# The layer norm at the start of a decode step's backward kernel moved to ScalarE, and its large clears divided between two engines

## The chip, the cores and the metric

The kernel runs on one core of one Trainium2 chip. The metric is the device time of one execution in microseconds (us), here the median of several runs. A profile records one further execution, in which every engine's instructions and every transfer have a start and a duration. TensorE is called PE, its weight load PEld, VectorE DVE, ScalarE ACT, GpSimd POOL and SyncE SP, as in the profile.

## The reference

The computation is one decode step of a transformer block, forward and backward together. Batch is 2, sequence 1, width D = 576; there are 32 query heads and 16 key/value heads of 128, a cache of 4096 positions, and a bilinear MLP of width F = 4608.

```python
def _layernorm(x, axis=-1, eps=1e-5):
    m = jnp.mean(x, axis=axis, keepdims=True)
    v = jnp.var(x, axis=axis, keepdims=True)
    return (x - m) / jnp.sqrt(v + eps)

def _A_ref(x, k_cache, v_cache, wq, wo):        # 2 query heads for each key/value head
    q = (x @ wq) as [B, Hq, 1, Dh]
    scores = einsum("bhqd,bhkd->bhqk", q, k) * (Dh ** -0.5)
    o = einsum("bhqk,bhkd->bhqd", softmax(scores), v)
    return o as [B, 1, Hq * Dh] @ wo

def _B_ref(x, w_gate, w_up, w_down):
    return ((x @ w_gate) * (x @ w_up)) @ w_down

xn = _layernorm(x)
out = x + _A_ref(xn, ...) + _B_ref(xn, ...)
```

The kernel returns `out` and its gradients, for the given `grad_out`, with respect to x, both caches, and the five weight matrices. The two cache gradients alone are 67 MB, as large as the caches that are read. All told 92.5 MB are read and 92.5 MB written.

## The kernel before

**Constants and the front.** A front of small work comes first. POOL clears `ident`, `xs`, `Wdy`, `W` (two of them), `dM`, `Wm`, `Wt`, `oT` and `rowT`, that is, stationary operands of which later steps overwrite only a part. DVE derives a dozen selection matrices from the identity (`identf`, `sel`, `selA`, `R4`, `G4`, `RV`, `F8`, `Q4`, `C32`, `mask8`, `maskc`; lines 130 to 159). The layer norm of the two rows of x then works on [2, 576] tiles: a cast to `x_f` (line 168), the row sum `mu` (171), the mean (172), the centred `xn_f` (174), its mean square `var` (177), `rstd` by ACT's square root (184) and DVE's reciprocal (185), the scaling (186), and the cast to `xn_bf` (188). PE spreads `dy_bf` and `xn_bf` over all partitions (`dyr`, `xnr`, lines 198 to 200) and transposes `xn_bf` into `xs` (207 to 212). `Wdy` is filled from the transposed `dyr` (220).

**Groups.** Four groups of four key/value heads follow. `group_loads` loads a slice of the query weights `wq` and of the output weights `wo`; `group_front` makes from them the query rows and the rows of the output's gradient (`qd`, lines 458 to 476, with `Wdy` as weights of the `wo` matmuls) and spreads them (`rep`, 485). `build_W` (496, POOL) puts them into the cleared `W`.

**Steps.** Each of the 16 steps handles two heads of one batch: it loads K (1 MB a head, line 520), transposes it on DVE (`X`, helper line 121), computes scores on PE (`ps_sc`), the softmax, then loads V and does the same for the probabilities' gradient. At the end of a step `contract` multiplies the probabilities with V (and their gradient with K one step later). The cache gradients are outer products that PE forms in `ps_o`; ACT or DVE evicts them (`so`, helper lines 112 and 109), and POOL issues their stores (585). Nine slices of the MLP are interleaved as units between them (`mlp_units`: `wgu` and `wd` are loaded at 316 to 319).

**What sets the order.** A tile framework schedules the instructions from the program's order and priorities; on each engine they run strictly in the order that it wrote out. All loads go through SP's queue in one order. The loaded tiles (`wq`, `wo`, `wgu`, `wd`, `kv`, and in the front `xn_f`) share 12 buffers of the tag `nat`, so that a load is issued only when the last reader of the tile that held its buffer is done; SP then stands at that load, and all later loads stand behind it:

```python
    def nat(shape, name):
        return sb.tile(list(shape), BF16, tag="nat", bufs=12, name=name)
```

Of the kernel before, what the change touches and what calls it, by code (L numbers as in the profile page):

```python
# [8 lines left out]
AF = mybir.ActivationFunctionType  # L9
ALU = mybir.AluOpType  # L10
AX = mybir.AxisListType
FP32 = mybir.dt.float32
# [11 lines left out]
def kernel(  # L24
# [22 lines left out]
    nc = tc.nc  # L47

    Bq, Sq, D = A_x.shape
# [20 lines left out]
    const = ctx.enter_context(tc.tile_pool(name="const", bufs=1))  # L70
# [86 lines left out]
    for be in range(4):  # L157
# [5 lines left out]
    x_bf = sb.tile([2, D], BF16, tag="st", bufs=5, name="x_bf")  # L163
# [1 line left out]
    dy_bf = sb.tile([2, D], BF16, tag="st", bufs=5, name="dy_bf")  # L165
    nc.sync.dma_start(dy_bf[:], grad_out.rearrange("b s d -> (b s) d"))
    x_f = sb.tile([2, D], FP32, tag="X", bufs=3, name="x_f")
    nc.vector.tensor_copy(x_f[:], x_bf[:])

    mu = const.tile([2, 1], FP32, name="mu")  # L170
    nc.vector.reduce_sum(mu[:], x_f[:], axis=AX.X)
    nc.vector.tensor_scalar(mu[:], mu[:], 1.0 / D, None, op0=ALU.mult)
    xn_f = sb.tile([2, D], FP32, tag="nat", bufs=12, name="xn_f")
    nc.vector.tensor_scalar(xn_f[:], x_f[:], mu[:], None, op0=ALU.subtract)
    xsq = sb.tile([2, D], FP32, tag="X", bufs=3, name="xsq")
    var = const.tile([2, 1], FP32, name="var")
    nc.vector.tensor_tensor_reduce(
        out=xsq[:], in0=xn_f[:], in1=xn_f[:], scale=1.0 / D, scalar=0.0,
        op0=ALU.mult, op1=ALU.add, accum_out=var[:],
    )  # L180
    eps_t = const.tile([2, 1], FP32, name="eps_t")
    nc.vector.memset(eps_t[:], EPS)
    rstd = const.tile([2, 1], FP32, name="rstd")
    nc.scalar.activation(rstd[:], var[:], AF.Sqrt, bias=eps_t[:], scale=1.0)
    nc.vector.reciprocal(rstd[:], rstd[:])
    nc.vector.tensor_scalar(xn_f[:], xn_f[:], rstd[:], None, op0=ALU.mult)
    xn_bf = sb.tile([2, D], BF16, tag="st", bufs=5, name="xn_bf")
    nc.vector.tensor_copy(xn_bf[:], xn_f[:])


    sel2 = const.tile([2, 4, 32], BF16, name="sel2")
# [21 lines left out]


    Wdy = const.tile([P, NB, 2, P], BF16, name="Wdy")
    nc.gpsimd.memset(Wdy[:], 0.0)
    dyT = sb.tile([P, 2 * NB, 32], BF16, tag="X", bufs=3, name="dyT")
    t32(dyT[:].rearrange("p k m -> p (k m)"), view(dyr[:], 0, P, 0, [[64, NB], [1, 2], [2, 32]]))
    for a in range(4):
# [2 lines left out]

    W = [const.tile([P, 4, 2, WW], BF16, name=f"W{t}") for t in range(2)]
    dM = const.tile([P, 2, 2, P], BF16, name="dM")
    for t in range(2):
        nc.gpsimd.memset(W[t][:], 0.0)
    nc.gpsimd.memset(dM[:], 0.0)
    Wms = [const.tile([P, 35, 8], BF16, name=f"Wm{i}") for i in range(2)]
    Wts = [const.tile([P, 19, 8], BF16, name=f"Wt{i}") for i in range(2)]
    oTs = [const.tile([P, 2, GH, 32], BF16, name=f"oT{i}") for i in range(2)]  # L230
# [693 lines left out]
```

## Time and profile before

| quantity | before |
|---|---|
| median of 5 runs | 520.44 us (518.93 to 536.76) |
| the 5 runs | 536.76, 520.44, 519.57, 531.47, 518.93 us |
| profiled execution: time | 519.58 us |
| profiled execution: span of its trace | 517.8 us |
| mean granted PE clock | 0.832 |
| busy: PE, DVE, ACT, POOL | 422.5, 359.5, 328.2, 204.6 us |
| bytes over the span | 186.26 MB, mean 360 GB/s |

The profile's time counts from the trace's start. Its busy times leave out the issuing of DMAs and waits. "Idle before, releaser" says how long an engine stood still before an instruction, and what ended it. "DMA share" is the mean busy share of the core's 16 DMA engines; it can read a little over 1 in a short stretch. 1.8 us of the execution's time lie outside the trace's span.

### The profile page before, as it was taken

The page shows a single profiled execution, that of the slowest core. Times are in us where ns is not written, and L with a number is a line of the kernel's source. Part 1 is how long each engine was busy: PE and PEld are TensorE (multiplying, and loading weights), DVE is VectorE, ACT ScalarE, POOL GpSimd, SP SyncE. Part 2 cuts the span into 40 slices and gives each one's busy share as a digit, 9 for nine tenths or more (in the row PEclk, how much of TensorE's full clock was granted, in tenths as well). Part 3 has the DMA queues.
Part 4 walks back from the last instruction along what each step waited for, and adds up shares of the span by engine and source line. Part 5 has one row for each costly group of instructions (what it writes and reads, how often), then busy time and mean ns, then how long its engine had stood idle before and what let it go on. Part 6 is the DMA issues. An engine that isn't in the chain of part 4 may idle for free.

```text
span 517.8 us, 20063 instructions
## 1 busy us (share of the span) xinstructions
PE 422.5 (82%) x8921; PEld 338.4 (65%) x8921; DVE 359.5 (69%) x624; ACT 328.2 (63%) x454; POOL 204.6 (40%) x372
## 2 busy tenths in 40 slices
PE   0587897988899887987899889879988878899872
PEld 0476776766777666776777767757777657777630
DVE  8689584638828958466586588748594859698464
ACT  1042888667756565687467774757777655788653
POOL 5023344333342543432433635353434255453313
PEclk9978989669959778687677995979897999899655
DMA  8994999999999999999898999999999999976646
GB/s 255 407 376 199 332 415 386 403 403 403 404 357 372 349 338 419 317 409 408 307 400 354 361 420 416 371 398 418 391 416 361 422 411 405 381 293 240 247 192 235
DMA packets 52911, 186.26 MB, mean 360 GB/s; under 512 B 4140, under 2 KB 19128, under 8 KB 44632
## 3 DMA queue, kind: packets, MB, share of 16 engines
q1 hardware_dynamic: 28392, 92.49, 47.9%
q0 software_dynamic: 24432, 92.48, 45.0%
q8 instruction: 70, 1.15, 0.9%
q14 instruction: 17, 0.14, 0.1%
HBM read 92.48 MB, written 92.48 MB: 357 GB/s over the span
## 4 chain that ended last, share of the span: by engine, by line
PE 46%; DVE 15%; ACT 15%; DMA 11%; issue 8%; SPq 3%; POOL 1%; POOLq 0%; DVEq 0%; ACTq 0%
PE ps_sc L93 18%; ACT so L112 12%; PE ps_o L93 12%; PE ps_m L93 10%; DVE X L121 6%; DMA kv<-in_A_k_cache_dram 5%; DMA wd<-in_B_w_down_dram 4%; DVE so L109 3%; SPq L317 2%; PE ps_m L558 2%; DMA kv<-in_A_v_cache_dram 2%; DMA wgu<-in_B_w_gate_dram 1%; DVE Xw L121 1%; PE ps_m L509 1%; PE ps_m L607 1%
## 5 line engine op out<-in xcount | busy, mean ns | idle before, releaser
L112 ACT CAST so<-ps_o 128x1024 bf16<-128x1024 f32 x232 | 225.6, 1022 | 62.8 <-PE ps_o L93 59.1
L121 DVE STREAM_TRANSPOSE X<-kv 128x1024 f32<-128x1024 f32 x128 | 157.4, 1233 | 52.5 <-PE ps_sc L93 46.7
L93 PE MATMUL ps_sc<-X,W 128*128 128x128 bf16 x2048 | 162.1, 238 | 13.5 <-issue 6.5
L93 PEld LDWEIGHTS <-W 128*128 128x128 bf16 x2048 | 144.4, 107 | 21.5 <-issue 14.8
L585 POOL DMA_DIRECT2D out_dram<-so x64 | 49.8, 778 | 122.5 <-ACT so L112 72.0
L93 PE MATMUL ps_o<-bd,dsm 32*128 32x128 bf16 x1024 | 48.1, 237 | 14.0 <-ACT so L112 8.7
L93 PE MATMUL ps_o<-bd,prm 32*128 32x128 bf16 x1024 | 45.7, 232 | 11.6 <-ACT so L112 4.8
L93 PEld LDWEIGHTS <-dsm 32*128 32x128 bf16 x1024 | 29.1, 101 | 28.7 <-issue 22.9
L93 PE MATMUL ps_m<-kv,rowT 128*32 128x128 bf16 x2048 | 43.5, 248 | 5.1 <-issue 4.4
L93 PEld LDWEIGHTS <-prm 32*128 32x128 bf16 x1024 | 27.4, 98 | 24.6 <-issue 18.4
L93 PEld LDWEIGHTS <-rowT 128*32 128x32 bf16 x2048 | 36.2, 111 | 8.2 <-issue 6.0
L112 ACT CAST stw<-ps_o 128x1024 bf16<-128x1024 f32 x28 | 28.0, 1021 | 19.7 <-PE ps_o L93 18.4
L496 POOL COPY W<-rep 32x16 bf16<-32x16 bf16 x128 | 24.6, 192 | 29.1 <-PE ps_sc L93 21.9
L564 POOL TENSOR_TENSOR prm<-pr,maskc 128x1024 bf16<-128x1024 bf16 x16 | 30.2, 1890 | 13.0 <-DVE pr L612 12.9
L564 POOL TENSOR_TENSOR dsm<-ds,maskc 128x1024 bf16<-128x1024 bf16 x16 | 30.3, 1894 | 9.4 <-DVE ds L632 8.9
L109 DVE CAST so<-ps_o 128x1024 bf16<-128x1024 f32 x24 | 28.7, 1194 | 3.3 <-PE ps_o L93 3.3
L396 POOL DMA_DIRECT2D out_dram<-stw x18 | 13.6, 757 | 34.5 <-ACT stw L112 17.6
L503 POOL COPY dM<-qd 128x128 bf16<-128x128 bf16 x32 | 9.1, 288 | 45.5 <-PE ps_m L509 28.3
L93 PEld LDWEIGHTS <-Wdy 128*128 128x128 bf16 x306 | 22.9, 113 | 4.6 <-POOL dM L503 3.0
L121 DVE STREAM_TRANSPOSE Xw<-wgu 128x1152 f32<-128x1152 f32 x18 | 24.5, 1364 | 1.9 <-PE ps_sc L93 1.8
L112 ACT CAST std<-ps_o 128x576 bf16<-128x576 f32 x36 | 22.2, 646 | 5.7 <-PE ps_o L93 4.1
L555 ACT COPY o_sb<-ps_m 128x128 f32<-128x128 f32 x32 | 8.6, 269 | 25.8 <-PE ps_m L93 25.6
(172 smaller groups left out, 559.0 us busy)
## 6 DMA issues: line engine op xcount, KB each, us to landing
out_dram<-so POOLq DMA_DIRECT2D x64, 1024.0 KB, 10.6
kv<-in_A_k_cache_dram SPq DMA_DIRECT2D x32, 1024.0 KB, 13.3
kv<-in_A_v_cache_dram SPq DMA_DIRECT2D x32, 1024.0 KB, 9.6
out_dram<-stw POOLq DMA_DIRECT2D x18, 512.0 KB, 9.4
wd<-in_B_w_down_dram SPq DMA_DIRECT2D x9, 576.0 KB, 11.1
out_dram<-std POOLq DMA_DIRECT2D x9, 576.0 KB, 9.8
wo<-in_A_wo_dram SPq DMA_DIRECT2D x4, 1152.0 KB, 14.7
wgu<-in_B_w_gate_dram SPq DMA_DIRECT2D x9, 512.0 KB, 17.7
```

What stands on the lines that cost most here:

```text
L93: ins = nc.tensor.matmul(*args, **kwargs)
L109: nc.vector.tensor_copy(out=out, in_=in_)
L112: nc.scalar.copy(out, in_)
L121: nc.vector.transpose(out, in_)
L317: nc.sync.dma_start(wgu[64 * w:64 * w + 64, 8], Wsrc[512:576, f0:f0 + FS])
L396: nc.gpsimd.dma_start(out[0:512, f0:f0 + FS].rearrange("(c p) n -> p c n", p=P), st[:])
L496: nc.gpsimd.tensor_copy(view(W[t][:], 32 * a, 32, 28 + 32 * a, [[2 * WW, 4], [WW + 2, 2], [1, 2]]), view(st["rep"][:], 32 * a, 32, t * 4 * ...
L503: nc.gpsimd.tensor_copy(view(dM[:], 0, P, t * 2 * P, [[P + 2, 2], [4, 32], [1, 2]]), view(st["qd"][:], 0, P, (2 if t == 0 else 1) * GH * 2 ...
L555: nc.scalar.copy(o_sb[:], o_ps[:])
L558: nc.tensor.matmul(t_ps[:], lhsT=o_sb[:], rhs=RV[:].rearrange("p x r -> p (x r)"), start=True, stop=True)
L564: nc.gpsimd.tensor_tensor(m[:], view(rows[:], 0, P, 0, [[0, 8], [1, P]]), view(maskc[:], 0, P, 0, [[1, 8], [0, P]]), ALU.mult)
L585: nc.gpsimd.dma_start(oview[b, :, :, l0 + x].rearrange("a m n -> m a n"), st[:].rearrange("p a c d -> p a (c d)"))
```

## The change

The layer norm's passes over [2, 576] move from DVE to ACT. A copy with a summed output gives `x_f` and the sum in one instruction. DVE makes two small values of the sum: the negative mean `negmu`, which the next step takes as its bias, and the mean `mu`, which the end of the kernel needs. ACT then centres (`xn_f`), squares with a summed output (`xsq`, `var`), takes the root, and after DVE's reciprocal scales and casts in one instruction (`xn_bf`). Three of the clears, `Wdy`, `dM` and the first `W`, move from POOL to DVE; the second `W` and the small tiles stay on POOL. The rest of the program's text is unchanged.

```diff
     x_f = sb.tile([2, D], FP32, tag="X", bufs=3, name="x_f")
-    nc.vector.tensor_copy(x_f[:], x_bf[:])
-
     mu = const.tile([2, 1], FP32, name="mu")
-    nc.vector.reduce_sum(mu[:], x_f[:], axis=AX.X)
+    negmu = const.tile([2, 1], FP32, name="negmu")
+    nc.scalar.activation(x_f[:], x_bf[:], AF.Copy, accum_out=mu[:])
+    nc.vector.tensor_scalar(negmu[:], mu[:], -1.0 / D, None, op0=ALU.mult)
     nc.vector.tensor_scalar(mu[:], mu[:], 1.0 / D, None, op0=ALU.mult)
     xn_f = sb.tile([2, D], FP32, tag="nat", bufs=12, name="xn_f")
-    nc.vector.tensor_scalar(xn_f[:], x_f[:], mu[:], None, op0=ALU.subtract)
+    nc.scalar.activation(xn_f[:], x_f[:], AF.Identity, bias=negmu[:], scale=1.0)
     xsq = sb.tile([2, D], FP32, tag="X", bufs=3, name="xsq")
     var = const.tile([2, 1], FP32, name="var")
-    nc.vector.tensor_tensor_reduce(
-        out=xsq[:], in0=xn_f[:], in1=xn_f[:], scale=1.0 / D, scalar=0.0,
-        op0=ALU.mult, op1=ALU.add, accum_out=var[:],
-    )
+    nc.scalar.activation(xsq[:], xn_f[:], AF.Square, accum_out=var[:])
     eps_t = const.tile([2, 1], FP32, name="eps_t")
     nc.vector.memset(eps_t[:], EPS)
     rstd = const.tile([2, 1], FP32, name="rstd")
-    nc.scalar.activation(rstd[:], var[:], AF.Sqrt, bias=eps_t[:], scale=1.0)
+    nc.scalar.activation(rstd[:], var[:], AF.Sqrt, bias=eps_t[:], scale=1.0 / D)
     nc.vector.reciprocal(rstd[:], rstd[:])
-    nc.vector.tensor_scalar(xn_f[:], xn_f[:], rstd[:], None, op0=ALU.mult)
     xn_bf = sb.tile([2, D], BF16, tag="st", bufs=5, name="xn_bf")
-    nc.vector.tensor_copy(xn_bf[:], xn_f[:])
+    nc.scalar.activation(xn_bf[:], xn_f[:], AF.Copy, scale=rstd[:])
...
-    nc.gpsimd.memset(Wdy[:], 0.0)
+    nc.vector.memset(Wdy[:], 0.0)
...
-    for t in range(2):
-        nc.gpsimd.memset(W[t][:], 0.0)
-    nc.gpsimd.memset(dM[:], 0.0)
+    nc.vector.memset(dM[:], 0.0)
+    nc.vector.memset(W[0][:], 0.0)
+    nc.gpsimd.memset(W[1][:], 0.0)
```

In the order of instructions that results, DVE starts with two one-column clears, then `Wdy` (as 1152 four-byte elements a partition), `dM` (256) and `W[0]` (624), then `negmu`, the clears of `acc` and `accx`, `mu`, the reciprocal, and the selection matrices in their old order. ACT has a table load ahead of the copy and a second one between the square and the root. On PE the four small matmuls that spread the queries (482) stand behind the gate and up matmuls instead of inside the `wo` matmuls. Everything else on every engine and on SP's queue stands in the order that it had.

## The prediction, made before the changed kernel was run

> **What bounds the kernel now.** I read the page's slices first. The 16 DMA engines are nine tenths busy or more in nearly every slice from the third to the thirty-fifth, except the fourth. The table of stretches shows the transfers' hole, and the middle:
>
> ```profile
> 42.00:44.00 2.00, 1.56 (x24) 1.27 (x22) 2.00 (x5) 0.85 (x1) 0.00 (x0) 1.00 1.00 406
> 44.00:46.00 2.00, 1.39 (x18) 1.20 (x17) 2.00 (x3) 0.00 (x0) 0.72 (x4) 1.00 0.52 199
> 46.00:48.00 2.00, 1.07 (x10) 1.07 (x11) 1.97 (x7) 0.76 (x3) 0.25 (x2) 0.77 0.04 12
> 48.00:50.00 2.00, 2.00 (x31) 1.99 (x33) 1.21 (x3) 0.07 (x1) 1.69 (x2) 0.50 0.00 0
> 50.00:52.00 2.00, 1.96 (x94) 1.66 (x86) 1.37 (x5) 0.80 (x2) 1.13 (x2) 0.88 0.03 8
> ...
> 240.00:280.00 40.00, 35.09 (x668) 28.54 (x666) 24.10 (x45) 26.33 (x39) 14.30 (x22) 0.70 0.95 371
> 320.00:360.00 40.00, 33.44 (x725) 27.74 (x726) 28.86 (x46) 25.72 (x37) 18.21 (x32) 0.87 1.02 395
> ```
>
> The last three columns are granted PE clock, DMA share and GB/s. From 44 to 52 us the transfers stand idle for 0.96 + 1.92 + 2.00 + 1.94 = 6.8 us; from 52 to 440 they hardly do (0.95 to 1.03 in stretches of 40 us). So the middle runs at the transfers' pace, PE close behind (33 to 36 us of 40), and time can be won where the transfers idle. Two views, SP's timeline and the chain of waits, say what ends the hole:
>
> ```profile
> 32.77 4.16 SPq L520 DMA_DIRECT2D kv<-in_A_v_cache_dram  x2
> 51.13 0.33 SPq L520 DMA_DIRECT2D kv<-in_A_k_cache_dram  x1
> ...
> 49.69 1.40 PE ps_m L93 x48
> ```
>
> The buffers are full. The next K load is issued at 51.13, just after the first step's contraction with V (49.69 to 51.09) has released a buffer. That contraction ends a chain of compute that starts with the layer norm. So the question is how much earlier that chain runs. DVE's timeline of the front:
>
> ```profile
> 0.94 0.19 DVE L245 MEMSET accx<- 128x160 f32 x1
> 2.08 6.37 DVE L168 CAST x_f<-x_bf 2x576 f32<-2x576 bf16 x1 [0.95 <-DMA x_bf<-in_A_x_dram]
> ...
> 11.10 0.15 DVE L185 RECIPROCAL rstd<-rstd 2x1 f32<-2x1 f32 x1 [0.36 <-ACT rstd L184]
> 11.29 0.51 DVE L186 TENSOR_SCALAR xn_f<-xn_f,rstd 2x576 f32<-2x576 f32 x1
> 11.83 0.45 DVE L188 CAST xn_bf<-xn_f 2x576 bf16<-2x576 f32 x1
> 12.20 0.21 DVE L130 CAST identf<-ident 128x128 f32<-128x128 bf16 x1
> ```
>
> A cast of 2x576 elements takes 6.37 us, ending at 8.45; the same cast near the kernel's end (line 780) takes 0.436. POOL's clears run back to back until 8.15 (`rowT`, 7.86 + 0.29). The cast was held until POOL had finished: 5.9 us of stall.
>
> **The change, part by part.** I follow DVE to the start of `identf`, at 12.20 before: 2.4 us of selection matrices stand behind it, then `xs`, `dyr`, `xnr` and all of `group_front`, in the old order. How far `identf` moves is how far the front moves.
>
> *POOL's clears.* By the spacing of their starts, `Wdy` (1.96), one `W` (1.08) and `dM` (0.46) leave POOL, so POOL ends at 8.15 - 3.50 = 4.65.
>
> *DVE's clears.* They start at 0.88, where `acc` started. Rows: one element takes 0.06 us, `accx` with 160 four-byte elements 0.19. At that slope (0.8 ns an element) 1152, 256 and 624 cost 1.0 + 0.3 + 0.6 = 1.9 us; in proportion to `accx` (1.2 ns) 2.4. They end between 2.7 and 3.3; I take 3.1. That needs them to run beside POOL: `accx` did (0.94 to 1.13, while POOL cleared `xs`, 0.89 to 1.15).
>
> *The copy with sum on ACT.* The first table load ends at 2.02, x lands at 2.05, so it starts at 2.08 as the cast did. No ACT row has two partitions; by the 128x576 row it costs 0.65, plus 0.1 for the part of the accumulator's read (0.206) that sticks out: done at 2.85. The clears thus hide it or stand over by up to 0.4 us.
>
> ```profile
> L112 ACT CAST std<-ps_o 128x576 bf16<-128x576 f32 x36 | 22.2, 646 | 5.7 <-PE ps_o L93 4.1 <-ACT stqt L112 0.7 <-ACT ex L605 0.3
> L555 ACT COPY o_sb<-ps_m 128x128 f32<-128x128 f32 x32 | 8.6, 269 | 25.8 <-PE ps_m L93 25.6
> L605 ACT ACTIVATE ex<-ps_sc,negb 128x128 f32<-128x128 f32 x16 | 6.0, 377 | 6.6 <-DVE negb L602 6.6
> L605 ACT ACT_TABLE_LOAD x1 | 1.3, 1283 | 0.0
> L605 ACT ACTIVATION_READ_ACCUMULATOR ex<-ps_sc,negb 128x1 f32 x16 | 3.3, 206 | 0.0
> ```
>
> *`negmu`, the new wait between the engines.* It costs 0.14 (`mu`, line 172); queued behind it on DVE are only `acc`, `accx`, `mu` and the reciprocal, and ACT waits for it. At 3.1 POOL is still clearing. If a one-column multiply goes through, it ends at 3.25; if it is held as the cast was, until 4.65, it ends at 4.8. No row decides. The nearest is another narrow multiply from SBUF to SBUF, line 459:
>
> ```profile
> L459 DVE TENSOR_SCALAR qd<-qd x4: 172/464/1564, 18.4 to 382.2; 128x16 bf16<-128x16 bf16 x4
> ```
>
> With 16 columns it takes 0.17 us at best and 1.56 at worst, so narrow multiplies are held too; I take 4.8.
>
> *The rest of the norm on ACT.* Centring takes 0.65 + 0.11 for a per-partition operand (377 against 269 at 128x128) = 0.75; squaring with its sum 0.75; the second table load 1.28; the root 0.29; DVE's reciprocal 0.15; five handovers at 0.04. That is 3.4 us from `negmu` to the end of the reciprocal: 4.8 + 3.4 = 8.2, where `identf` starts. Lines 186 and 188 no longer stand between. `xn_bf` on ACT (0.75) ends at 9.0 and PE's transposes (0.5) at 9.5, inside the 2.4 us of selection matrices.
>
> So `identf` moves from 12.20 to 8.2: **4.0 us earlier**; with `negmu` unheld, to 6.65: 5.55 earlier.
>
> Here two pages of the Trainium skill are weighed. The rows give a table load 1283 ns, and none can show a delay behind one: line 605's first exponential waited for `negb` until long after its load. ScalarE: Activation LUTs, What ACT_TABLE_LOAD costs, adds about 1.38 us of drain to a switch; by it the estimate for the front would be about 2.6 us earlier instead of 4.0. SBUF — State Buffer, in its list of practical consequences on the shared ports, lets DVE's `copy`, `cast` and `tensor_scalar` contend with POOL when they run in a two-port mode, which supports holding `negmu` but not the clears.
>
> *Does it carry?* Downstream the loads must be there 4.0 to 5.6 us earlier. SP's waits show it: `wo` had landed by 10.80 (needed at 18.46 before), the gate and up weights by 15.12 (24.27), the first K by 18.75 (26.03), the second by 25.96 at the latest (33.63). Slack is 7 us or more everywhere. The moved PE matmuls (482) cost nothing net: 0.29 us leave the path to `dof`, and about as much is added ahead of `rep`. So the contraction and the K load at 51.13 move to 47.1. The transfers issued by then still drain near 44 to 45, as they were saturated, so the hole shrinks from 6.8 to about 2.8 us. Work issued one for one earlier then ends earlier, through the tail as well.
>
> Sum: 519.58 - 4.0 = 515.6 us. The profiled execution stands for the runs: 519.58 against 518.93, 519.57 and 520.44, the median of all five being the last. Forecast: **515.6**.
>
> **Rivals.** *`negmu` is not held.* 519.58 - 5.55 = 514.0. For it: a column has one element, and `mu` at 0.14 shows no hold (though POOL was idle). The hole would allow up to 6.8 us, so 512.8 is the floor.
>
> *More is late in the front.* Either DVE's clears are held until 4.65 too (`negmu` then at 4.65 + 2.2 + 0.15 = 7.0, `identf` at 10.4, 1.8 us gained), or ACT's table loads delay what follows by about as much again as a load (1.28: 2.7 us gained). 516.9 to 517.8. Against the first: `accx` ran beside POOL.
>
> *The gain is not kept.* The middle absorbs it, for instance by holding later buffers to another pace: 519.6. For it: SP waits 147 us in all for outer products (`ps_o`), so compute sets the issue of many loads. Against: that compute is earlier too.
>
> *Slower, by PE's clock.* PE works 422.5 us at a mean granted clock of 0.832, so 0.01 less costs about 422.5 x 0.01 / 0.832 = 5.1 us if all of it were on the path; the matmuls there are 46% of the chain, hence 2.3 us. An earlier, denser start could bring half-clock stretches onto the steps of the middle. From a mean clock below 0.815 (4.0 / 2.3 x 0.01 lost) the gain is gone, and at 0.805 the time is 522. Against it: in 240 to 280 the clock was 0.70 and PE was busy no longer, 35.09 us, with the transfers at 0.95.
>
> **How the numbers follow.** Chances: forecast 0.40 (514.9 to 516.5), `negmu` free 0.23, more late 0.15, not kept 0.12, slower 0.10. About 0.3% (1.6 us) is what a measurement of this kernel can tell from no change, so faster means below 518.0: the first three cases, 0.78, less 0.03 for the edge of the third, 0.75. Same: 0.12 + 0.03 = 0.15; slower 0.10. For the range I take the floor of the second case, 512.8, and up to 519.8, which takes in the case without gain and leaves the slower one out.
>
> **What would show it.** In the changed profile: `x_f` at 2.08 with about 0.65 on ACT; DVE's clears ending near 3.1; `negmu` lasting 1.6 us (held) or 0.14 (free); POOL's last clear ending near 4.65; `identf` near 8.2; the K load of 51.13 near 47.1; the transfers' hole down to about 3 us; stretches from 52 us as full as before. The working is wrong if `identf` comes later than 10.5, if the hole shrinks but the span does not, or if the mean clock falls below 0.815.

## The result, and the profile after

The changed kernel is faster by about one per cent in two comparisons of three. In the first comparison the ratio of its times to those of the kernel before is 0.9898 (95% interval 0.9874 to 0.9922), from 44 and 79 runs with medians of 517.53 and 523.03 us. Single runs spread by 20 us, and the ratios here take those within 1.5% of each kernel's fastest run. Two later comparisons with 12 runs each, e6 and e11 below, gave 0.9888 (0.9834 to 0.9942) and 1.0008 (0.9961 to 1.0056). Weighted by their intervals the three make 0.9915, so 4.4 us of 519.6. The third shows no gain, and it lies further from the other two than its interval and theirs allow; so the uncertainty is nearer to half of their spread, 0.006 to either side (1.3 to 7.5 us), than to the 0.002 that the weighting gives. The medians of all runs give 0.9895, 1.0007 and 0.9922: which of the later two shows the gain depends on the measure.

The profiled execution took 515.75 us with a span of 514.0, against 519.58 and 517.8 before; the mean granted clock is 0.851 against 0.832.

The front first. VectorE's timeline and ScalarE's timeline of the changed kernel (start, duration, both in us):

```profile
1.12 1.02 DVE L212 MEMSET Wdy<- 128x1152 uint32 x1 [0.22 <-issue]
2.14 0.27 DVE L221 MEMSET dM<- 128x256 uint32 x1
2.49 0.58 DVE L222 MEMSET W<- 128x624 uint32 x1
2.98 0.08 DVE L171 TENSOR_SCALAR negmu<-mu 2x1 f32<-2x1 f32 x1
...
6.34 0.15 DVE L182 RECIPROCAL rstd<-rstd 2x1 f32<-2x1 f32 x1 [3.00 <-ACT rstd L181]
6.43 0.20 DVE L130 CAST identf<-ident 128x128 f32<-128x128 bf16 x1
```

```profile
2.08 0.68 ACT L170 ACTIVATE x_f<-x_bf 2x576 f32<-2x576 bf16 x1
2.67 0.18 ACT L170 ACTIVATION_READ_ACCUMULATOR x_f<-x_bf 2x1 f32 x1
3.13 0.77 ACT L174 ACTIVATE xn_f<-x_f,negmu 2x576 f32<-2x576 f32 x1 [0.27 <-DVE negmu L171]
3.93 0.68 ACT L177 ACTIVATE xsq<-xn_f 2x576 f32<-2x576 f32 x1
4.52 0.19 ACT L177 ACTIVATION_READ_ACCUMULATOR xsq<-xn_f 2x1 f32 x1
4.72 1.28 ACT L181 ACT_TABLE_LOAD   x1
6.02 0.29 ACT L181 ACTIVATE rstd<-var,eps_t 2x1 f32<-2x1 f32 x1
```

`identf` starts at 6.43 instead of 12.20: the front is 5.8 us earlier. The copy that took 6.37 us on VectorE takes 0.68 on ScalarE. VectorE's three clears end at 3.07, beside GpSimd's, and `negmu` goes through at once.

SP's timeline and the table of stretches (PE clock, DMA share and GB/s last) answer to the hole:

```profile
43.52 0.33 SPq L516 DMA_DIRECT2D kv<-in_A_k_cache_dram  x1
```

```profile
44.00:46.00 2.00, 1.95 (x90) 1.68 (x91) 0.74 (x3) 1.52 (x2) 1.67 (x1) 1.00 0.93 328
46.00:48.00 2.00, 1.66 (x32) 1.36 (x25) 0.18 (x1) 2.00 (x4) 0.23 (x1) 1.00 0.95 380
48.00:50.00 2.00, 2.00 (x69) 1.62 (x68) 1.80 (x3) 1.70 (x5) 0.84 (x2) 1.00 1.08 343
50.00:52.00 2.00, 2.00 (x45) 1.77 (x42) 1.42 (x3) 1.60 (x3) 1.35 (x3) 1.00 1.12 339
```

The K load that stood at 51.13 is issued at 43.52, 7.6 us earlier, and the transfers no longer pause: between 42 and 56 us their idle time (shares above one counted as one) is 0.24 us instead of 7.08.

### The profile page after: what moved, and what is told of

Its sections match the earlier page's. It is cut to its first block, busy times and chain, and to the rows that moved or that the text cites. A ratio compares the mean times of both kernels' runs of the same rounds, so it can differ in the third digit from the quotient of the medians.

```text
span 514.0 us, 20060 instructions
## 1 busy us (share of the span) xinstructions
PE 414.9 (81%) x8921; PEld 331.8 (65%) x8921; DVE 352.4 (69%) x621; ACT 332.3 (65%) x461; POOL 201.9 (39%) x369
## 4 chain that ended last, share of the span: by engine, by line
PE 27%; DMA 12%; ACT 9%; DVE 7%; issue 5%; SPq 3%; POOL 1%; POOLq 0%; ACTq 0%; DVEq 0%
PE ps_sc L93 9%; PE ps_o L93 7%; ACT so L112 7%; PE ps_m L93 7%; DMA out_dram<-so 7%; DMA out_dram<-sto 3%; SPq L313 2%; DVE X L121 2%; DMA wd<-in_B_w_down_dram 2%; DVE so L109 2%; PE ps_m L554 1%; ACT stw L112 1%; DVE sto L109 1%; PE ps_o L800 0%; ACT sto L112 0%
## 5 line engine op out<-in xcount | busy, mean ns | idle before, releaser
L93 PE MATMUL ps_sc<-X,W 128*128 128x128 bf16 x2048 | 156.5, 233 | 11.2 <-issue 5.3
L93 PEld LDWEIGHTS <-W 128*128 128x128 bf16 x2048 | 138.8, 105 | 19.1 <-issue 12.5
L93 PEld LDWEIGHTS <-xnr 32*128 32x128 bf16 (+1 forms) x440 | 13.7, 102 | 20.2 <-issue 16.2
```

The source lines that it names most:

```text
L93: ins = nc.tensor.matmul(*args, **kwargs)
```

## The experiments

The theory was that GpSimd's back-to-back clears held VectorE's cast, and that a front that ends earlier pays by closing the hole in the transfers. The first rival is that ScalarE's share is the whole gain and the clears do not matter; the second, that the front does not matter to the end at all.

**e1: the layer norm on ScalarE, the clears back on GpSimd.**

```diff
-    nc.vector.memset(Wdy[:], 0.0)
+    nc.gpsimd.memset(Wdy[:], 0.0)
...
-    nc.vector.memset(dM[:], 0.0)
-    nc.vector.memset(W[0][:], 0.0)
-    nc.gpsimd.memset(W[1][:], 0.0)
+    for t in range(2):
+        nc.gpsimd.memset(W[t][:], 0.0)
+    nc.gpsimd.memset(dM[:], 0.0)
```

> The layer norm on ScalarE, all clears back on GpSimd. Theory (the clears on GpSimd hold VectorE's wide copies and casts, and the front's lead shrinks the transfers' hole): GpSimd's clears end at 8.15 us again; the one-column negmu passes at about 3.0 and the reciprocal ends near 6.4, as in the changed kernel, but the 128x128 cast identf is held and ends only after 8.15; the K load comes near 45 to 47, the hole is 1 to 3 us; ratio to before about 0.992. Rival (the gain is ScalarE's alone, and the clears' place does not matter): identf at 6.4 and the whole gain, ratio 0.990.

Measured: 0.9933 (0.9888 to 0.9977). VectorE's timeline:

```profile
2.99 0.14 DVE L171 TENSOR_SCALAR negmu<-mu 2x1 f32<-2x1 f32 x1 [1.86 <-ACT x_f L170]
6.38 0.15 DVE L182 RECIPROCAL rstd<-rstd 2x1 f32<-2x1 f32 x1 [3.08 <-ACT rstd L181]
6.46 1.76 DVE L130 CAST identf<-ident 128x128 f32<-128x128 bf16 x1
```

The norm is as early as in the changed kernel, but now `identf` is held: 1.76 us instead of 0.20, to 8.22, just after GpSimd's last clear (7.86 + 0.29). The norm alone does not bring the whole lead.

**e2: the clears divided, the layer norm on VectorE as before.** Its edit is the other half of the change's diff.

> The clears divided, the layer norm on VectorE as before. Theory: the cast x_f is held only until GpSimd's end at 4.65, so it takes about 2.9 us instead of 6.37; two of VectorE's clears stand between the norm's steps; dyT at about 13.5 instead of 16.7, so about 3.3 us earlier, ratio about 0.994. Rival (ScalarE's share is the whole gain): the cast still takes about 6.4 us, ratio 1.000.

Measured: 0.9964 (0.9915 to 1.0014), so by time alone not told from no change. The cast is held until GpSimd is done, now at 4.64, and takes 2.71 us; `dyT` starts at 13.12 (expected 13.5):

```profile
2.23 2.71 DVE L168 CAST x_f<-x_bf 2x576 f32<-2x576 bf16 x1
```

**e3 and e4: e1 with clears that nothing needs.** They delay the front without changing the order of the other instructions on VectorE, ScalarE, PE and SP.

```diff
     nc.gpsimd.memset(dM[:], 0.0)
+    for _ in range(4):                      # e4: 10
+        nc.gpsimd.memset(W[1][:], 0.0)
```

> As e1, with four more clears of the second W on GpSimd, 1.08 us each, that nothing needs. Theory: GpSimd ends near 12.5, identf ends just after it, the front stands as late as before though the norm is done on ScalarE by 7.3; the hole is back at about 6 to 7 us; ratio about 1.000. Rival (no hold by GpSimd's clears): as the changed kernel, ratio 0.990.

> As e1, with ten more clears of the second W on GpSimd. Theory: GpSimd ends near 19, identf just after, 6.5 us later than before; the K load near 57, the hole near 13 us; ratio about 1.012: the front's delay is carried to the end one for one. Rival (the middle absorbs the front, the gain came from PE's clock): identf late, but ratio within 0.995 to 1.003.

Measured: e3 1.0006 (0.9963 to 1.0049), e4 1.0092 (1.0040 to 1.0144). In e4 seven of the ten clears stood between GpSimd's other clears of the front, so that it ended these at 15.7, not 19; the other three stood among its later copies, from 28.33 to 32.92. VectorE's timelines, of e3 and then of e4:

```profile
6.28 0.15 DVE L182 RECIPROCAL rstd<-rstd 2x1 f32<-2x1 f32 x1 [3.08 <-ACT rstd L181]
6.36 6.20 DVE L130 CAST identf<-ident 128x128 f32<-128x128 bf16 x1
```

```profile
6.35 0.15 DVE L182 RECIPROCAL rstd<-rstd 2x1 f32<-2x1 f32 x1 [3.08 <-ACT rstd L181]
6.43 9.37 DVE L130 CAST identf<-ident 128x128 f32<-128x128 bf16 x1
```

The norm stays fast on ScalarE, yet the whole gain is gone in e3, and e4 is slower than before. So the clears' end is what the front waits for, and the front's place carries to the end. In one table (`dyT` is the same transpose in all six; idle is that of the transfers from 42 to 56 us, each from one profile; of e3, whose profiled execution took 529.07 us, only these first 56 us are read):

| kernel | `dyT` starts, us | K load, us | transfers idle, us | ratio to before |
|---|---|---|---|---|
| changed | 10.94 | 43.52 | 0.2 | 0.9898 |
| e1, norm alone | 12.52 | 45.17 | 1.5 | 0.9933 |
| e2, clears alone | 13.12 | 46.58 | 2.8 | 0.9964 |
| before | 16.73 | 51.13 | 7.1 | 1 |
| e3, four clears more | 16.85 | 51.09 | 7.4 | 1.0006 |
| e4, ten clears more | 20.09 | 53.37 | 7.2 | 1.0092 |

From the changed kernel to e4 the front moves by 9.15 us and the ratio by 0.0194, that is 10.1 us of 519.6: near one for one, in the same order of kernels throughout, though the intervals of neighbours overlap. The firmest pair is e1 and e4, timed together against the same 35 runs of the kernel before: 7.6 us of front, and 0.0159 or 8.3 us of time. Both rivals fall. In e4 the hole does not grow, it only moves: the K load is 2.2 us later than before though `dyT` is 3.4 later, and its time, 4.8 us longer (2.1 to 7.5), is more than the idle of this stretch explains. Its three late clears also stood ahead of GpSimd's `W` copies and its first store, and whether they cost time isn't shown. So the front's place is shown to set the time, but in e4 this hole alone does not account for it.

**e5 and e10: a still shorter norm.** The root's table is loaded once at the start, the sum of squares no longer waits for the mean, and one instruction centres, scales and casts.

```diff
+    nc.scalar.activation(one_s[:], one1[:], AF.Sqrt)
     nc.scalar.activation(x_f[:], x_bf[:], AF.Copy, accum_out=mu[:])
...
+    nc.scalar.activation(xsq[:], x_bf[:], AF.Square, accum_out=var[:])
     nc.vector.tensor_scalar(mu[:], mu[:], 1.0 / D, None, op0=ALU.mult)
...
+    nc.vector.tensor_tensor(musq[:], mu[:], mu[:], ALU.mult)
+    nc.vector.scalar_tensor_tensor(out=var[:], in0=var[:], scalar=1.0 / D, in1=musq[:], op0=ALU.mult, op1=ALU.subtract)
...
+    nc.vector.scalar_tensor_tensor(out=negmu[:], in0=mu[:], scalar=-1.0, in1=rstd[:], op0=ALU.mult, op1=ALU.mult)
...
+    nc.scalar.activation(xn_bf[:], x_bf[:], AF.Identity, bias=negmu[:], scale=rstd[:])
```

> The changed kernel with a shorter norm: the square root's table is loaded once, ahead of everything, the sum of squares is taken of x beside the sum (variance as mean square less squared mean), and one ScalarE instruction scales and shifts. The reciprocal should end near 4.6 instead of 6.49 and identf start at about 4.7, where GpSimd's clears end; the front is about 1.7 us earlier than in the changed kernel, the K load near 42. Theory (the lead pays by the transfers' hole, which the changed kernel has closed): no more to win, ratio to before 0.988 to 0.991, as the changed kernel beside it. Rival (compute sets the pace through the middle, the hole only shows it): another 1.7 us, ratio about 0.9865.

> The kernel of e5 again, beside the changed kernel, since e5 (0.9948, interval 0.9906 to 0.9991) and e6 (0.9888, 0.9834 to 0.9942) overlap. Theory (the transfers' hole is closed, no more to win): the same ratio as the changed kernel within the intervals, about 0.990. Rival: lower than the changed kernel by 0.003.

Beside them ran the changed kernel itself, without an edit:

> The changed kernel itself, beside e5 on the same chip. Both theories: ratio to before about 0.990; its granted clock between 30 and 60 us shows whether the stretch without half clock in its first profile comes back.

> The changed kernel once more, beside e10 on the same chip. Both theories: a ratio to before of about 0.990, as in the first comparison.

Measured: e5 0.9948 (0.9906 to 0.9991) beside e6 0.9888 (0.9834 to 0.9942); e10 0.9974 (0.9907 to 1.0041) beside e11 1.0008 (0.9961 to 1.0056). The two pairs point opposite ways; by their intervals the mean is 0.9955 for the shorter norm and 0.9956 for the changed kernel in these pairs. No difference is seen, but the rival's 0.003 is not excluded. The trace shows where part of the lead, 1.7 us at `dyT` (9.24 against 10.94), goes. VectorE's timeline of e5:

```profile
11.45 2.64 DVE L121 STREAM_TRANSPOSE Xo<-wo 128x1152 f32<-128x1152 f32 x2 [0.46 <-DMA wo<-in_A_wo_dram]
...
20.71 2.37 DVE L121 STREAM_TRANSPOSE X<-kv 128x1024 f32<-128x1024 f32 x2 [1.53 <-DMA kv<-in_A_k_cache_dram]
```

It now waits for `wo` and for the first K, whose transpose starts at 20.71; in the changed kernel it starts at 20.58. There the shorter norm ran ahead of its loads, and the lead was handed back. In e10, the same kernel, it waited for `wo` alone (0.30 us); the first K's transpose started at 19.62 without a wait, and 1.0 us of the lead was left.

**e7: the centring on VectorE, in the changed kernel.** It was to tell when a multiply or add by a scalar is held.

```diff
-    nc.scalar.activation(xn_f[:], x_f[:], AF.Identity, bias=negmu[:], scale=1.0)
+    nc.vector.tensor_scalar(xn_f[:], x_f[:], negmu[:], None, op0=ALU.add)
```

> The changed kernel with the centring (a 576-column tensor_scalar) on VectorE instead of ScalarE. If the hold by GpSimd's clears depends on the operation's width and not on its kind (negmu, one column, the same operation, passed in 0.08 us while GpSimd cleared), it starts at about 3.3 and ends only just after GpSimd's end at 4.65, 1.3 to 1.6 us long instead of 0.51, and the reciprocal ends near 7.2. If narrow and wide are alike, it takes 0.51 and the reciprocal ends near 6.3.

Measured: not held. It takes 0.51 us at 3.28, with all its 576 columns, and it is a GpSimd clear that waits: `oT` takes 1.30 us for its pair instead of 0.99. GpSimd's timeline of e7:

```profile
3.09 0.39 POOL L228 MEMSET Wt<- 128x152 bf16 x2
3.42 1.30 POOL L228 MEMSET oT<- 128x512 bf16 x2
```

**e8 and e9: the kind of operation, or the moment?** e8 is e1 with e7's edit, so that the centring arrives inside a long clear. e9 is the kernel before with its held cast written as a multiplication.

```diff
-    nc.vector.tensor_copy(x_f[:], x_bf[:])
+    nc.vector.tensor_scalar(x_f[:], x_bf[:], 1.0, None, op0=ALU.mult)
```

> All clears on GpSimd as in e1, and the centring on VectorE as in e7. The 576-column tensor_scalar then arrives near 3.2 us, inside GpSimd's long clear of Wdy (1.46 to 3.48). If the kind of operation decides (multiplies by a scalar are never held, casts are), it takes 0.51 us again. If the moment decides and VectorE gets its turn at the next boundary between two clears, it ends near 4.0, 0.8 us long. If an operation that arrives during a clear is held until GpSimd has nothing more to clear, it ends near 8.6, over 5 us long.

> The kernel before with the cast x_f written as a multiplication by 1.0 (bf16 to fp32, the same 2x576 elements, the same place). If the kind of operation decides, it takes about 0.5 us at 2.08 instead of 6.37 and the front is 5.9 us earlier. If the moment of arrival decides, inside the clear of Wdy, it takes about 6.4 as the cast did.

VectorE's timelines, of e8 and then of e9:

```profile
3.13 1.74 DVE L174 TENSOR_SCALAR xn_f<-x_f,negmu 2x576 f32<-2x576 f32 x1
...
7.39 0.45 DVE L130 CAST identf<-ident 128x128 f32<-128x128 bf16 x1
```

```profile
2.08 2.78 DVE L168 TENSOR_SCALAR x_f<-x_bf 2x576 f32<-2x576 bf16 x1 [0.95 <-DMA x_bf<-in_A_x_dram]
...
5.85 0.87 DVE L174 TENSOR_SCALAR xn_f<-x_f,mu 2x576 f32<-2x576 f32 x1
```

GpSimd's timeline of e9, where the clears ran on until 9.03:

```profile
1.47 2.02 POOL L216 MEMSET Wdy<- 128x2304 bf16 x1
3.42 2.53 POOL L226 MEMSET W<- 128x1248 bf16 x2
5.90 0.52 POOL L227 MEMSET dM<- 128x512 bf16 x1
```

Each wide multiply was held, but got its turn while GpSimd still had clears to do: in e8 and e9 it ended at 4.87 and 4.86, a little after the first `W` clear, and the two `W` clears took 2.53 us together instead of 2.22. The same 2x576 cast in the same place had been held to 8.45. So neither of the plain answers holds: the multiply is held by the running clear and the next, not by all. Nor is every cast held to the end: e8's `identf` took 0.45 us at 7.39 while GpSimd cleared until 8.67. What decides who gets the next turn stays open. e9 took 518.17 us, e7 514.27 and e8 513.71, each in a single run; single times say nothing here.

## Why the prediction was right, step by step

**What held.** The stall was GpSimd's, as read from the cast's 6.37 us: e2, e3 and e4 move its end with the clears' end. GpSimd's clears ended at 4.65 as worked out. VectorE's end at 3.07 (3.1 taken), beside GpSimd. The copy with its sum was done at 2.85, exactly as summed from the 128x576 eviction and the accumulator's read. From `negmu` to the end of the reciprocal it took 3.43 us (3.06 to 6.49), 3.4 forecast. The root started 0.02 us after its table load ended; here the 1.38 us of drain that the Trainium skill (ScalarE: Activation LUTs, What ACT_TABLE_LOAD costs) adds to a switch do not show, and the rows' 1.28 us were the whole price.

**The step that was mis-sized** is `negmu`: taken as held until 4.65, from the nearest row (line 459, 16 columns, 0.17 to 1.56 us), it passed in 0.08 us, in e1 in 0.14. The row's 1.56 us were a hold, but of sixteen columns and by one running product: in the kernel before it lasted from 382.15 to 383.71, and GpSimd's `prm` (line 564) from 381.80 to 383.69. It said nothing of a single column beside clears. So the front moved by 5.8 us and not by 4.0: it was the rival "not held" that came for the front. Its price for the time, 514.0, compares with 0.9898 x 519.58 = 514.3; by the weighted 0.9915 it is 515.2, near the forecast's 515.6 by luck: more front was gained, and less of it shows in the time, than the sum had.

**The K load came earlier than the front.** It moved by 7.6 us; the other 1.8 came between. The table of stretches of before shows PE at half clock around the first scores and again around 48:

```profile
28.00:30.00 2.00, 2.00 (x22) 2.00 (x20) 1.95 (x3) 0.48 (x1) 0.90 (x1) 0.50 1.07 329
30.00:32.00 2.00, 2.00 (x22) 2.00 (x20) 1.67 (x2) 0.00 (x0) 0.00 (x0) 0.50 1.14 303
```

In the changed kernel the first such stretch is shorter (0.63 in 22 to 24, 0.52 in 24 to 26, then 1.00), and the second, 0.50 in 48 to 50 before, does not come before 60 us. Nothing in the steps foresaw it. e6 and e11, the same kernel, also show a mean clock of 0.83 in 20 to 30 and 1.00 in 30 to 40, and issue this K load at 43.96 and 44.26, so the three are 6.9 to 7.6 us earlier; in e11 a second half-clock stretch comes at 44 to 46 (0.50). The kernel before has one profile only, but e3, whose front stands as late, has the long stretch too (0.62, 0.50, 0.50 and 0.67 from 26 to 34). An early front does not by itself bring the short one: e5 and e7 have 0.67 and 0.66 in 20 to 30. e5 and e10, one kernel, issue this K load at 44.27 with the long stretch and at 42.56 with the short one. What sets its length isn't shown.

**The hole closed; how much of it was kept can't be read from a profile.** The hole was forecast at 2.8 us and is 0.2. Of its 6.8 us and the K load's 7.6, the two profiles keep 3.8 in the span. Their transfers were busy for 93.9% of 517.8 us and 94.3% of 514.0 (the queues' shares added), hence idle for 31.6 and 29.3 us: of the hole's 6.8 us, 4.5 came back as idle later, 0.92 in the stretch from 400 to 440 us where it had been 1.01. e6's profile has 95.2% of 506.2, 24.3 us idle, and 1.02 in that stretch. So the idle of the middle differs from run to run by more than the gain, and the profile of one run can't tell what is kept; the ratios, 0.9898 to 0.9915 for 5.8 us of front (5.3 to 4.4 us) and the table above, say that most is, within the uncertainty of the ratios. What sets the middle's idle in a given run wasn't found.

**The slower rival's price is seen between runs, but not its cause.** Of the changed kernel's 44 runs the 15 with a clock below 0.82 (mean 0.808) took 522.8 us on average, the 9 above 0.835 (mean 0.850) 513.0: 9.8 us for 0.042, 2.3 us for 0.01, as the rival was priced. The two go together; which drives which isn't shown. That the clock did not fall through the change can't be said: the two profiles have 0.851 against 0.832, but the mean over the runs of e6 and e11 is 0.829 and 0.822, with 0.837 and 0.830 for the kernel before beside them. A fall of 0.008 is within the spread of these runs; at the rival's price it would cost 1.8 us.

**The slack of the loads was read too large, by e5.** Seven microseconds were taken for the first K from SP's waits. e5 shows its transposes waiting until 20.71, 5.3 us ahead of before (26.03), when the front is 7.5 us earlier at `dyT`; the changed kernel, 5.8 us earlier, starts them at 20.58 without a wait, and e10 at 19.62. So the loads' arrival differs from run to run by at least a microsecond, and the change took all of the lead that they allow in e5, and all but a microsecond or so in e10.

## What to carry to other kernels

An instruction that takes ten times what its like takes elsewhere in the same trace is waiting inside its own bar, and the neighbour to look for is the one that ends with it: here GpSimd's clears. Before a front is shortened, look for a hole in the transfers behind it, which a lead can fill, though the time followed the front in e4 without the hole growing; and compare the lead with the arrival of the loads that the front needs, because past that point a shorter chain only waits (e5). Where runs spread by 4%, several variants that move one event by known amounts say more than one pair of times.

## What the runs showed of the hardware

VectorE's casts of bf16 to fp32 were held by back-to-back GpSimd clears until the last one had ended in five profiles (6.37 us before, 2.71 in e2, 1.76, 6.20 and 9.37 for `identf` in e1, e3 and e4), in e4 across seventeen clears with no turn between them; but not in e8, where `identf` took 0.45 us at 7.39 while GpSimd cleared until 8.67. A multiplication by a scalar of the same size in the same place got in after two clears (2.78 in e9), a one-column multiply was not held at all (0.08 to 0.14), nor were VectorE's own clears (1.02, 0.27 and 0.58 us, beside GpSimd's). The Trainium skill (SBUF — State Buffer, in its list of practical consequences) says that, when VectorE runs in a two-port mode, whoever issues first gets the shared ports for the whole instruction and the other blocks. e7 agrees, with GpSimd's `oT` clears longer by 0.31 us while VectorE ran; but one whole instruction does not explain a cast that lost to a whole series of them, nor its difference from the multiply.
